# Large SBUF buffers laid out ahead of the small ones, so that TensorE's operands start at multiples of 512 bytes

## The chip, the cores and the metric

One NeuronCore of a Trainium2 chip runs one program. The metric is device time in microseconds (us). Before the change the median of three runs is 1743.22 us, with 1742.43 and 1743.45 us at the ends. The profiled execution took 1742.54 us, of which 1740.5 us lie between its first and its last instruction (its span).

## The reference

Chunked attention feeds a dense two-layer network, which feeds a mixture of eight experts:

```python
# q, k, v: 8 batches, 8 heads, 576 rows of 64; attention inside chunks of 64 rows
scores = scale * q_c @ k_c.T ; scores -= max
attn = exp(scores) / (sum + 1e-9)
x = (attn @ v_c) -> 4608 tokens x 512
h = x @ w_in ; x = (h - tanh(h)) @ w_out          # 512 -> 2048 -> 512
noisy = x @ w_gate + log1p(exp(x @ w_noise)) * noise
top 2 of 8 experts for each token, softmax over the two
out += weight * (relu(x[mask] @ w1[e]) @ w2[e])   # 512 -> 1024 -> 512, for each expert
```

All of it is float32. The kernel reaches float32 accuracy with three matmuls where one would do: each operand is split into a high part, rounded to the format `fp32r`, and a low part that holds the rest, and high x high, high x low and low x high are summed in PSUM.

## The kernel before

**Tiling.** A token tile is 128 tokens, and 36 tiles make 11 groups of the first network: 4, 3, 4, 3, 4, 3 tiles, and then five groups of 3. For each group the kernel runs 16 steps, one for each 128 hidden units. A step is a first layer (`products1`, line 331: 12 matmuls, each of 512 or 384 columns, as many as the group has tokens) and a second layer (`products2`, line 439: 3 matmuls for each token tile, each of 512 columns). The experts follow with the same two lines: 8 experts, each with three groups of 512, 384 and at most 352 tokens (in another order for odd and even experts), 8 steps for a group. Where an expert got so few tokens that its last tile is empty, the group of 352 runs as 256.

**Software pipeline.** `advance` issues the first layer of a step, and then the second layer of the step before it. Thus matmuls of line 331 and of line 439 alternate in blocks. Between blocks there are slots, filled by an explicit table, in which the attention of later tiles, the gating and the preparation of weights are issued. In the part of the experts TensorE runs the two lines alone.

**The four operands.** A matmul has a stationary operand (`lhsT`, loaded by an LDWEIGHTS instruction) and a moving operand (`rhs`, streamed):

```python
nc.tensor.matmul(s.hp[:, :n], lhsT=w[:, a, d, :], rhs=s.xt[:, b, d, :n], ...)            # line 331
nc.tensor.matmul(s.grp["acc"][j][:m], lhsT=s.gt[:, a, j * 128:j * 128 + m],
                 rhs=s.B[s.f][:, b, :], ...)                                               # line 439
```

In the first layer the stationary operand is a weight tile `wa` (128 columns of 4 bytes, thus 512 bytes in a partition), the moving one is the transposed input `xt`. In the second layer the stationary one is the activation `gt`, the moving one is the weight tile `wb`. `xt` is two buffers: groups with an even number use `xt0` (512 columns to a part), odd ones `xt1` (384 columns). `gt` is two buffers in rotation. The last group's eight steps are different: their activations are kept, under the name `gl`, in buffers of the tag `wa`, and their second layer runs at the very end, tile by tile (`by_tiles`), first the tile of 96 tokens and then the two of 128.

**Where a tile lies.** A pool gives its buffers their addresses in the order in which their tags are first asked for. In the pool `sp` the sixteen `wa`, the sixteen `wb` and three working buffers come first. What follows is asked for as the program comes to it, and small tiles (`mx`, 2 x 32 bytes, and `sm`, 2 x 32 bytes) are asked for between large ones. Addresses are bytes within a partition.

Of the kernel before, what the change touches and what calls it, by code (L numbers as in the profile page):

```python
# [10 lines left out]
F32R = mybir.dt.float32r  # L11
# [19 lines left out]
def moe_chain_kernel(ctx: ExitStack, tc: tile.TileContext, q, k, v, w_in, w_out, wgn, noise,  # L31
# [15 lines left out]
    sp = ctx.enter_context(tc.tile_pool(name="sp", bufs=1))  # L47
# [46 lines left out]
    def blk(name, tag, bufs, dt=F32):  # L94
        return sp.tile([128, 512], dt, name=name, tag=tag, bufs=bufs)
# [7 lines left out]
    def spare(tag, f):  # L103
        return raws[tag][f].bitcast(F32)
# [13 lines left out]
    def load_v(i):  # L118
        V[i] = spare("wb", NF1 - 2)[:, i % 2] if 2 <= i < GS[0] else blk("v", "v", 2)
        nc.sync.dma_start(V[i], v[i])  # L120

    PS, MX, PT, PX, LO = {}, {}, {}, {}, {}

# [70 lines left out]
    def p_mm(i):  # L194
        PX[i] = place_of(i, 0)
        products(PX[i], V.pop(i), PT.pop(i))
        if GS[0] <= i + 2 < NT:
            load_v(i + 2)
# [40 lines left out]
    def u_p_chunk(i, c):  # L239
        if c == 0:  # L240
            PX[i] = one_bank()
        products(PX[i], V[i], PT[i], (c,))
        g, j = place[i]
        if i == G0[g] and c == 0:
            XT[g] = new_xt(g, 128 * GS[g])
        s0 = j * 128 + 64 * c
        hi, lo = [XT[g][:, b, :, s0:s0 + 64] for b in range(2)]
        nc.scalar.copy(hi, PX[i][:, c])
        nc.vector.tensor_tensor(lo, PX[i][:, c], hi.bitcast(F32), op=ALU.subtract)
        if c == 1:  # L250
            for d in (V, PT, PX):
                d.pop(i)
            load_v(i + 2)
# [570 lines left out]
    for i in range(GS[0]):  # L824
        load_q(i)
        load_k(i)
        if i == 1:
            load_v(0)
# [249 lines left out]
    for g in range(NG):  # L1078
        h0 = H1 * g
        at(h0, load_nz, g)  # L1080
        if g > 0:
            n = GS[g - 1]
# [177 lines left out]
```

## Time and profile before

| | |
|---|---|
| median of three runs | 1743.22 us |
| profiled execution | 1742.54 us |
| its span | 1740.5 us |
| TensorE busy with matmuls | 1728.3 us (99%) |
| TensorE loading weights | 1485.9 us (85%) |
| VectorE, ScalarE, GpSimd busy | 790.6, 547.5, 491.7 us |
| DMA | 184.68 MB, mean 106 GB/s |

How to read it: matmuls are pipelined, so the duration of one (some 395 ns for 512 columns) overlaps the next ones, and a busy TensorE says nothing of its rate. The rate is read from the timeline, which merges instructions of one kind that follow each other: the start of a block, taken from the start of the next block, over the number of matmuls in it is the time from one matmul to the next, called the pitch here.

### The profile page before, as it was taken

What the parts mean: (1) busy time and instruction counts of PE and PEld (TensorE: products, weight loads), DVE (VectorE), ACT (ScalarE), POOL (GpSimd) and SP (SyncE); (2) the same over time, 40 slices, a digit from 0 to 9 for tenths busy, and PEclk for the clock granted to TensorE, in tenths of its full rate; (3) what the DMA queues carried; (4) which work ended last, traced back from release to release, by engine and by line L of the source; (5) the groups of instructions that cost most, each with busy time, mean ns of one, the idle gap of its engine ahead of it and who ended that gap; (6) DMA issues with size and microseconds to landing.
All of it is one profiled execution on the core that took longest, in us unless ns stands there. A gap on an engine that the chain in (4) does not pass through costs nothing.

```text
span 1740.5 us, 28351 instructions
## 1 busy us (share of the span) xinstructions
PE 1728.3 (99%) x10776; PEld 1485.9 (85%) x10777; DVE 790.6 (45%) x2070; ACT 547.5 (31%) x1108; POOL 491.7 (28%) x752
## 2 busy tenths in 40 slices
PE   8999999999999999999999999999999999999998
PEld 6788888888888888888898888988898888988887
DVE  8866443644454544544465333434333333343321
ACT  5643322332232333323342323323223222232211
POOL 4640403040304213031253523222232222232112
PEclk9999999999999999999999999999999999999999
DMA  8546525571323222121354543543354353443312
GB/s 315 182 128 161 163 63 155 126 206 43 107 79 113 82 79 101 55 95 38 112 175 120 130 108 79 106 106 68 87 103 104 73 96 85 93 111 71 65 25 37
DMA packets 197830, 184.68 MB, mean 106 GB/s; under 512 B 80176, under 2 KB 139568, under 8 KB 197680
## 3 DMA queue, kind: packets, MB, share of 16 engines
q1 hardware_dynamic: 178064, 142.73, 27.5%
q0 software_dynamic: 19328, 39.41, 11.8%
q8 instruction: 96, 1.57, 0.4%
q14 instruction: 54, 0.44, 0.1%
q10 hardware_dynamic: 288, 0.52, 0.1%
HBM read 118.76 MB, written 63.84 MB: 105 GB/s over the span
## 4 chain that ended last, share of the span: by engine, by line
PE 97%; DVE 1%; ACT 0%; POOL 0%; issue 0%; POOLq 0%; ACTq 0%; DVEq 0%
PE hp L331 47%; PE acc L439 46%; PE pair L136 2%; PE pt L190 1%; PE one L136 0%; PE pair L538 0%; PE acc L519 0%; PE hp L820 0%; DVE sm L172 0%; DVE e L156 0%; PE pair L519 0%; POOL out_dram L794 0%; DVE mx L149 0%; DVE g L370 0%; ACT xt L206 0%
## 5 line engine op out<-in xcount | busy, mean ns | idle before, releaser
L331 PE MATMUL hp<-xt,wa 128*128 128x384 f32 (+3 forms) x4416 | 879.3, 348 | 0.9 <-ACT xt L206 0.9
L439 PE MATMUL acc<-wb,gt 128*128 128x512 f32 x3432 | 859.0, 395 | 0.0
L331 PEld LDWEIGHTS hp<-xt,wa 128*128 128x128 f32 x4416 | 765.2, 188 | 82.9 <-issue 2.6
L439 PEld LDWEIGHTS acc<-wb,gt 128*128 128x128 f32 x3432 | 636.3, 188 | 131.0
L378 DVE SCALAR_TENSOR_TENSOR gt<-hp,gt 128x384 fp32r<-128x384 f32 (+2 forms) x184 | 109.2, 593 | 437.3 <-ACT gt L375 437.3
L375 ACT ACTIVATE gt<-hp 128x384 fp32r<-128x384 f32 (+2 forms) x184 | 95.6, 520 | 445.9 <-PE hp L331 426.0
L370 DVE TENSOR_TENSOR g<-hp,g 128x384 f32<-128x384 f32 (+1 forms) x176 | 104.1, 592 | 249.9 <-ACT g L367 249.3
L367 ACT ACTIVATE g<-hp 128x384 f32<-128x384 f32 (+1 forms) x176 | 91.4, 519 | 335.5 <-PE hp L331 330.8
L316 POOL TENSOR_TENSOR wb<-st,wb 128x512 fp32r<-128x512 f32 x64 | 92.9, 1451 | 321.5 <-ACT wb L314 321.5
L373 DVE TENSOR_TENSOR gt<-g,gt 128x384 fp32r<-128x384 f32 (+1 forms) x160 | 94.1, 588 | 96.0 <-ACT gt L371 95.5
L371 ACT CAST gt<-g 128x384 fp32r<-128x384 f32 (+1 forms) x176 | 95.4, 542 | 130.3 <-DVE g L370 116.2
L794 POOL DMA_INDIRECT out_dram<-o,lsa x73 | 119.3, 1634 | 53.4 <-DVE o L791 31.3
L396 POOL COPY spacer<-mark 1x1 f32<-1x1 f32 x182 | 47.2, 260 | 304.3 <-DVE mark L391 237.8
L613 POOL TENSOR_SCALAR r<-d 128x3 f32<-128x3 f32 (+1 forms) x11 | 3.3, 297 | 425.5 <-ACT d L604 425.4
L664 POOL DMA_INDIRECT xs<-yr,row x72 | 71.2, 988 | 32.0 <-issue 25.1
L269 DVE TENSOR_TENSOR xt<-xg,xt 128x512 fp32r<-128x512 f32 x80 | 54.3, 679 | 54.7 <-ACT xt L268 54.7
L268 ACT CAST xt<-xg 128x512 fp32r<-128x512 f32 x80 | 48.8, 610 | 91.6 <-DVE xg L491 90.1
L664 POOL DMA_INDIRECT lst<-pay,row x72 | 70.2, 975 | 16.1 <-issue 14.0
L491 DVE STREAM_TRANSPOSE xg<-xg 128x512 f32<-128x512 f32 x80 | 56.3, 704 | 0.0
L316 DVE TENSOR_TENSOR wa<-st,wa 128x512 fp32r<-128x512 f32 x64 | 44.1, 688 | 5.5 <-ACT wa L314 5.4
L314 ACT CAST wa<-st 128x512 fp32r<-128x512 f32 x64 | 39.3, 613 | 4.6 <-DMA st<-in_w_dram 4.6
L314 ACT CAST wb<-st 128x512 fp32r<-128x512 f32 x64 | 39.7, 620 | 0.4 <-DMA st<-in_w_dram 0.4
(197 smaller groups left out, 896.3 us busy)
## 6 DMA issues: line engine op xcount, KB each, us to landing
st<-in_w_dram SPq DMA_DIRECT2D x128, 256.0 KB, 2.9
xg<-xs SPq DMA_DIRECT2D x320, 64.0 KB, 2.4
out_dram<-zero SPq DMA_DIRECT2D x40, 256.0 KB, 4.5
x2d<-y SPq DMA_DIRECT2D x36, 256.0 KB, 2.3
z<-x2d SPq DMA_DIRECT2D x144, 64.0 KB, 2.1
yr<-x2d SPq DMA_DIRECT2D x36, 256.0 KB, 4.5
q<-in_q_dram SPq DMA_DIRECT2D x34, 256.0 KB, 4.1
v<-in_v_dram SPq DMA_DIRECT2D x34, 256.0 KB, 3.6
```

The source lines that it names most:

```text
L314: nc.scalar.copy(w[:, 0, :], x)
L316: eng.tensor_tensor(w[:, 1, :], x, w[:, 0, :].bitcast(F32), op=ALU.subtract)
L331: nc.tensor.matmul(s.hp[:, :n], lhsT=w[:, a, d, :], rhs=s.xt[:, b, d, :n], start=(i == 0), stop=(i == 11))
L367: nc.scalar.activation(g, hp[:, :n], AF.Tanh)
L370: nc.vector.tensor_tensor(g, hp[:, :n], g, op=ALU.subtract)
L371: nc.scalar.copy(hi, g)
L373: eng.tensor_tensor(lo, g, hi.bitcast(F32), op=ALU.subtract)
L375: nc.scalar.activation(hi, hp[:, :n], AF.Relu)
L378: nc.vector.scalar_tensor_tensor(lo, hp[:, :n], 0.0, hi.bitcast(F32), op0=ALU.max, op1=ALU.subtract)
L439: nc.tensor.matmul(s.grp["acc"][j][:m], lhsT=s.gt[:, a, j * 128:j * 128 + m], rhs=s.B[s.f][:, b, :], start=(s.f == 0 and i == 0), stop=(s. ...
L664: s = nc.gpsimd.indirect_dma_start(out=to, out_offset=bass.IndirectOffsetOnAxis(ap=at, axis=0), in_=src, in_offset=None)
L794: a = nc.gpsimd.indirect_dma_start(out=out, out_offset=bass.IndirectOffsetOnAxis(ap=en[:m, 0:1], axis=0), in_=o[:m], in_offset=None, compu ...
```

## The change

Five requests for tiles are put ahead of the small ones. The tiles that they return are not used: the requests only fix where the tags lie.

```diff
@@ -118,6 +118,12 @@
     def load_v(i):
         V[i] = spare("wb", NF1 - 2)[:, i % 2] if 2 <= i < GS[0] else blk("v", "v", 2)
         nc.sync.dma_start(V[i], v[i])
+
+    for n, m in ((0, 512), (1, 384)):
+        sp.tile([128, 2, 4, m], F32R, name=f"xt{n}", bufs=1)
+    sp.tile([128, 2, 512], F32R, name="gt", bufs=2)
+    blk("e", "e", 2)
+    blk("y", "y", 4)
 
     PS, MX, PT, PX, LO = {}, {}, {}, {}, {}
```

The built program holds the same instructions on each engine, in the same order, with the same waits and the same shapes. Every buffer keeps its users; what differs is the address of these (the small ones, of 4 to 128 bytes, move behind them):

| buffer | bytes | address before | mod 512 | address after | mod 512 |
|---|---|---|---|---|---|
| `wa` x16, `wb` x16, `xg`/`ks`/`pts` | 4096 each | 19456 to 158720 | 0 | the same | 0 |
| `xt0` | 16384 | 187520 | 128 | 162816 | 0 |
| `xt1` | 12288 | 212480 | 0 | 179200 | 0 |
| `gt` x2 | 4096 each | 203904, 208000 | 128 | 191488, 195584 | 0 |
| `e` x2 | 2048 each | 175168, 177216 | 64 | 199680, 201728 | 0 |
| `y` x4 (also `z`, `x`, `o`, `yr`, `x2t`) | 2048 each | 179328 to 185472 | 128 | 203776 to 209920 | 0 |
| `g`, `q` x2, `v` x2, `x2t` | 2048 each | 162816 to 173056 | 0 | 211968 to 222208 | 0 |

## Rows read from the trace of the kernel before

**Rows 1.** The page, part 1: busy us (share of the span) and instructions.

```profile
PE 1728.3 (99%) x10776; PEld 1485.9 (85%) x10777; DVE 790.6 (45%) x2070; ACT 547.5 (31%) x1108; POOL 491.7 (28%) x752
```

**Rows 2.** The page, part 4: the chain that ended last, by engine.

```profile
PE 97%; DVE 1%; ACT 0%; POOL 0%; issue 0%; POOLq 0%; ACTq 0%; DVEq 0%
```

**Rows 3.** TensorE's waits: who waited for whom, us in total, times, longest.

```profile
PE hp L820 <- DVE warm L814: 1.3, 1, 1.3
...
PE pair L136 <- DMA wa<-in_k_dram: 0.4, 1, 0.4
```

**Rows 4.** Groups of TensorE's matmuls by shape: count | busy us, mean ns.

```profile
L439 PE MATMUL acc<-wb,gt 128*128 128x512 f32 x3408 | 855.8, 395 | 0.0
...
L331 PE MATMUL hp<-xt,wa 128*128 128x352 f32 x192 | 32.3, 322 | 0.0
...
L439 PE MATMUL acc<-wb,gl 128*128 128x512 f32 x48 | 11.0, 389 | 0.0
```

**Rows 5.** TensorE's timeline, experts' groups of 384 and 512: start us, us, what.

```profile
1317.31 2.27 PE L331 MATMUL hp<-xt,wa 128*128 128x384 f32 x12
1319.42 2.25 PE L439 MATMUL acc<-wb,gt 128*128 128x512 f32 x9
1321.51 2.27 PE L331 MATMUL hp<-xt,wa 128*128 128x384 f32 x12
...
1352.98 2.96 PE L331 MATMUL hp<-xt,wa 128*128 128x512 f32 x12
1355.78 2.96 PE L439 MATMUL acc<-wb,gt 128*128 128x512 f32 x12
1358.57 2.96 PE L331 MATMUL hp<-xt,wa 128*128 128x512 f32 x12
```

**Rows 6.** TensorE's timeline at the end (the second from 1722.5 us on).

```profile
1716.72 16.57 PE L439 MATMUL acc<-wb,gl 128*96 128x512 f32 x72
...
1722.25 11.04 PE L439 MATMUL acc<-wb,gl 128*128 128x512 f32 x48
```

**Rows 7.** TensorE's timeline from 1318.7 us: the last six of that block.

```profile
1318.38 1.20 PE L331 MATMUL hp<-xt,wa 128*128 128x384 f32 x6
```

**Rows 8.** TensorE's timeline, first network, a block of 384 that reads xt0.

```profile
757.58 2.27 PE L331 MATMUL hp<-xt,wa 128*128 128x384 f32 x12
759.69 2.26 PE L439 MATMUL acc<-wb,gt 128*128 128x512 f32 x9
```

**Rows 9.** TensorE's timeline: where experts 2 and 4 begin.

```profile
1107.85 2.27 PE L331 MATMUL hp<-xt,wa 128*128 128x384 f32 x12
...
1309.62 2.27 PE L331 MATMUL hp<-xt,wa 128*128 128x384 f32 x12
```

**Rows 10.** Stretches: length, PE, PEld, DVE, ACT, POOL busy (instructions), PEclk, DMA.

```profile
1107.85:1309.62 201.77, 201.77 (x1010) 173.91 (x1009) 72.67 (x164) 59.43 (x116) 56.88 (x56) 1.00 0.43 94
50.00:100.00 50.00, 50.00 (x321) 39.04 (x320) 41.93 (x79) 30.58 (x58) 31.88 (x26) 1.00 0.53 189
```

**Rows 11.** Timeline in the first group: TensorE, and GpSimd's weight preparation.

```profile
65.25 3.05 PE L439 MATMUL acc<-wb,gt 128*128 128x512 f32 x12
68.13 2.95 PE L331 MATMUL hp<-xt,wa 128*128 128x512 f32 x12
...
63.66 1.29 POOL L316 TENSOR_TENSOR wa<-x,wa 128x512 fp32r<-128x512 f32 x1 [0.32 <-ACT wa L314]
66.85 1.30 POOL L373 TENSOR_TENSOR gt<-g,gt 128x512 fp32r<-128x512 f32 x1 [1.90 <-ACT gt L371]
```

**Rows 12.** TensorE's timeline, blocks of 352: xt1, and then xt0.

```profile
1386.54 2.10 PE L331 MATMUL hp<-xt,wa 128*128 128x352 f32 x12
1388.48 2.96 PE L439 MATMUL acc<-wb,gt 128*128 128x512 f32 x12
...
1703.42 13.46 PE L331 MATMUL hp<-xt,wa 128*128 128x352 f32 x84
```

## The prediction

> **What bounds the kernel now.** The page's busy shares come first: matmuls keep TensorE busy for 1728.3 us, 99% of the span, and no other engine passes 45% [rows 1]. The chain that ended last says the same from the other side: 97% of it is TensorE [rows 2]. Then TensorE's waits: the longest is 1.3 us, for the very first operand, and the only one on a transfer is 0.4 us [rows 3]. So the kernel ends when TensorE has pushed its matmuls through, and the one thing worth asking is the pitch, the time from one matmul to the next. The clock was granted in full, the 2.4 GHz level, in the stretches that I use [rows 10], so a matmul of n columns streams for n / 2.4 ns: 213.3 ns for 512, 160.0 ns for 384.
>
> The pitch is read from block starts. In the experts' groups of 512 a first-layer block of 12 and a second-layer block of 12 take 1358.57 - 1352.98 = 5.59 us: 232.9 ns a matmul, 19.6 ns over the streaming time. In a group of 384 the 12 of the first layer take 1319.42 - 1317.31 = 2.11 us (175.8 ns, 15.8 over) and the 9 of the second layer 2.09 us (232.2 ns, 18.9 over) [rows 5]. These excesses are not waits; they are there in every block.
>
> Two places show another pitch. At the very end the last 48 matmuls take 11.04 us from the first start to the last end; less the 0.389 us of the last one [rows 4] that is 10.65 us for 47 pitches: 226.6 ns, 13.3 over [rows 6]. These are the same second-layer matmuls with the same `wb`, but the stationary operand is `gl`, which lies at a multiple of 512 bytes, while `gt` lies 128 bytes past one. And in the group of 384 that reads `xt1` (`xt1` and `wa` both at multiples of 512) the first six of a block take 1318.38 - 1317.31 = 1.07 us, 178.3 ns each, but the last six 1.04 us, 173.3 ns each, again 13.3 over [rows 5, 7]; the first six follow second-layer matmuls that loaded a `gt` out of place. A block that reads `xt0` (128 past) stays at 2.11 us for 12 [rows 8]. My reading: with both operands at multiples of 512 the excess settles at 13.3 ns; with one 128 bytes off it wanders around 16 to 20 ns.
>
> **The change part by part.** No instruction, wait or queue place is added or moved; only addresses differ. Three kinds of edits follow.
>
> *gt, xt0 and xt1.* Every first-layer and second-layer matmul then has both operands at multiples of 512. The term is (pitch now - settled pitch) x count, with 226.6 ns for 512 columns, 173.3 for 384, and by the same 13.3 over streaming 160.0 for 352 and 120.0 for 256. Before the change no row shows 512 columns in the first layer with `xt` in place, so there the 226.6 of the end is carried over. Its bounds: at most the 6.3 ns down to 226.6 plus another 2 ns, since one block (352 columns on `xt0`) runs as low as 11.6 over; at the other end 3.4 ns worse (the slower case below).
>
> - Experts. From the start of expert 2 to that of expert 4 lie 201.77 us [rows 9], in which TensorE runs lines 331 and 439 alone: 192 first-layer matmuls each of 512, 384 and 256 columns and 432 of the second layer, 1008 in all (1010 with the two cut by the edges) [rows 10]. Settled they take 624 x 226.6 + 192 x 173.3 + 192 x 120.0 = 141.4 + 33.3 + 23.0 = 197.7 us. That is 4.1 us less for two experts, 16.2 us for eight.
> - First network. A step of a group of four has 24 matmuls of 512: 24 x (232.9 - 226.6) = 0.151 us, and 3 x 16 = 48 steps give 7.3 us. A step of three has 4.20 us [rows 5] against 12 x 173.3 + 9 x 226.6 = 4.12 us: 0.081 us, and 8 x 16 = 128 steps give 10.4 us. Together 17.6 us. Here attention and gating put small matmuls between the blocks, and the block behind them carries a stumble of its own that stays: 12 second-layer matmuls take 68.13 - 65.25 = 2.88 us in the first group [rows 11], against 2.80 in the experts [rows 5]. The steps touched by this gain less, and I take four fifths: 14 us.
>
> *e, y and the buffers that share their tags.* VectorE, ScalarE, GpSimd and the DMA queues work on them. None of these is on the chain for 2% [rows 2], so a change of either sign in their durations is hidden behind matmuls: zero, up to 1 us either way for the transposes and attention products.
>
> *The small buffers, and `g`, `q`, `v`, `x2t`.* The latter were at multiples of 512 and stay so. Zero.
>
> **What could be late next.** A faster TensorE leaves the others less time. The tightest place is the first group, where VectorE is busy for 41.93 of 50 us [rows 10] decoding weights. There GpSimd has finished the weight tile of a later step at 64.95 us, and its first use is at 68.13 [rows 11]: 3.2 us of cover, while the whole group would gain 16 x 0.15 = 2.4 us. GpSimd also waits 1.90 us for the activation that TensorE feeds [rows 11], so it is itself paced by TensorE. I charge nothing; if the cover were used up, at most these 2.4 us would be lost.
>
> **The sum.** 16.2 + 14 = 30 us from the profiled execution's 1742.54 gives 1712.5 us; the median of the runs is 0.7 us higher. I forecast 1713 us.
>
> **The rivals.**
>
> *Half of it.* Lying in place may not be enough to settle. For it: the last group's 24 matmuls with a stationary operand of 96 columns take 1722.25 - 1716.72 = 5.53 us, 230.4 ns each, though both operands lie at multiples of 512 [rows 6]; and a block of 352 on `xt1`, in place, takes 1388.48 - 1386.54 = 1.94 us, 161.7 ns, 15.0 over [rows 12]. If blocks that follow small matmuls, 256 columns or 96-column tiles do not settle, some half of the gain is left: 1728 us. Against it: behind the 96-column tiles the 48 of 128 columns run at 226.6.
>
> *Nothing.* The 226.6 at the end could come from quiet: by then the other engines have almost no work in SBUF, and the address would not matter. Then the second layer keeps 232 and the time stays at 1743 us, within 1 or 2. Against it: the last six of the block in [rows 7] settle in the middle of the experts, with VectorE, ScalarE and GpSimd each busy for about 30% [rows 10], while the first layer on `xt0` with 512 columns never does.
> The Trainium skill, page "TensorE: Matmul & The Clock Gate", section "Step-by-step: what each phase is for", also speaks for nothing: the streamed operand and the weight load have a read port each, so loading the next weights takes no read bandwidth from the running matmul, and where the two operands lie relative to each other should be free. The same page, section "Wait — 56ns, not 53.3ns?", puts consecutive warm matmuls at the streaming time plus about 2.5 ns. The trace does not agree with that figure in any block: 13.3 ns at best, 19.6 in the groups of 512 [rows 5, 6]. By that rule the sum would be zero; by the rows it is 30 us.
>
> *Slower.* Operands that all start alike could meet in the same part of the memory on every pass. For it: 84 matmuls of 352 columns on `xt0`, out of place, take 1716.72 - 1703.42 = 13.30 us, 158.3 ns each [rows 6, 12], 3.4 ns less than the block on `xt1`, in place, at 161.7. If that is the rule and the other rows the exception, the 3408 second-layer matmuls [rows 4] and the 2304 of the first layer that read `xt0` (6 of 11 groups with 16 blocks of 12, 12 of 24 with 8) lose 3.4 ns each: 19.4 us, 1762 us. It decides if the step of 512 comes out above 5.59 us. Against it: the in-place block followed out-of-place `gt` loads, and the counts of 352 are small (192 [rows 4]).
>
> *The change does not do what it says.* The requests stand before the program's first small ones in that pool, and the addresses of the built program are those of the table; I give it no chance of its own.
>
> **How the numbers follow.** The forecast, a gain of 25 to 36 us (1707 to 1718), 0.62. Half of it, a gain of 8 to 25 us, 0.22. Nothing, 0.10. Slower, 0.06. A measurement of this kernel tells a change from none at about 0.2%, 3.5 us. Faster by more than that is the first two: 0.84; within it 0.10; slower 0.06. The range takes the forecast's own 1707 to 1718, a microsecond below it for excesses under 13.3 ns, and reaches up into the half case until no more than two tenths are left out: 1706 to 1733.
>
> **What would show it.** The experts' step of 512 takes 5.44 us instead of 5.59, the step of 384 4.12 instead of 4.20, and two experts 197.7 us instead of 201.8. First- and second-layer blocks of 12 with 512 columns both take 2.72 us. A block of 384 takes 2.08 us from its first matmul on. The blocks of 352 on `xt0` get slightly longer (160 ns a matmul, from 158.3). The last 48 matmuls do not change. The prediction fails if the second layer keeps 232 ns with `gt` in place (the end is special then), if only one of the two layers settles, or if TensorE shows waits on weights in the first 100 us.

## The result, and the profile after

The changed kernel takes 1726.05 us (median of five runs, 1725.13 to 1726.58) against 1743.22 us for the kernel before in the same comparison: a ratio of 0.9902, 95% interval 0.9891 to 0.9912. The profiled execution has a span of 1723.1 us, 17.4 us shorter than before. It is faster, by a little over half of what was forecast.

The page still describes the same kernel: the same number of instructions, and TensorE bound [rows 1, 2]. VectorE, ScalarE and GpSimd are busy for the same time within 1 us. Busy us (share) and instructions, then the chain that ended last:

```profile
PE 1710.9 (99%) x10776; PEld 1484.3 (86%) x10777; DVE 790.0 (46%) x2070; ACT 547.5 (32%) x1108; POOL 490.7 (28%) x752
...
PE 97%; DVE 1%; ACT 0%; POOL 0%; issue 0%; POOLq 0%; ACTq 0%; DVEq 0%
```

So the time went inside TensorE's own sequence, and the blocks tell where. By shape (count | busy us, mean ns), two groups of the kernel before beside [rows 4], and then the same three of the changed one:

```profile
L331 PE MATMUL hp<-xt,wa 128*128 128x384 f32 x2304 | 438.6, 338 | 0.0
L331 PE MATMUL hp<-xt,wa 128*128 128x512 f32 x1344 | 331.9, 395 | 0.9 <-ACT xt L206 0.9
...
L445 PE MATMUL acc<-wb,gt 128*128 128x512 f32 x3408 | 846.3, 393 | 0.0
L337 PE MATMUL hp<-xt,wa 128*128 128x384 f32 x2304 | 437.7, 338 | 0.0
L337 PE MATMUL hp<-xt,wa 128*128 128x512 f32 x1344 | 324.5, 390 | 0.9 <-ACT xt L212 0.9
```

The second layer is 9.5 us shorter, the first layer of 512 columns 7.4 and that of 384 columns 0.9. TensorE's timeline in the same experts as [rows 5] (start us, us, what; lines 337 and 445 are 331 and 439 of before):

```profile
1313.34 2.27 PE L337 MATMUL hp<-xt,wa 128*128 128x384 f32 x12
1315.44 2.24 PE L445 MATMUL acc<-wb,gt 128*128 128x512 f32 x9
1317.53 0.51 PE L337 MATMUL hp<-xt,wa 128*128 128x384 f32 x2
...
1340.29 2.88 PE L337 MATMUL hp<-xt,wa 128*128 128x512 f32 x12
1343.01 2.88 PE L445 MATMUL acc<-wb,gt 128*128 128x512 f32 x12
1345.72 0.39 PE L337 MATMUL hp<-xt,wa 128*128 128x512 f32 x1
```

In the group of 512 a step now takes 1345.72 - 1340.29 = 5.43 us, 226.3 ns a matmul; it was 5.59 [rows 5]. That is the settled step of 5.44 us within a hundredth. In the group of 384 a step takes 1317.53 - 1313.34 = 4.19 us, where 4.12 was forecast and 4.20 was there before. The second layer's 9 matmuls take 2.09 us, as before, although `gt` is in place now. The next block's last six and what follows, from a narrower window:

```profile
1318.59 1.20 PE L337 MATMUL hp<-xt,wa 128*128 128x384 f32 x6
1319.63 0.63 PE L445 MATMUL acc<-wb,gt 128*128 128x512 f32 x2
```

The first six take 1318.59 - 1317.53 = 1.06 us, 176.7 ns each, and the last six 1.04 us, 173.3 ns each: the picture of [rows 5, 7] with both operands of every matmul in place.

The sums agree. Where experts 2 and 4 begin, and where the first network begins and ends:

```profile
19.33 0.96 PE L337 MATMUL hp<-xt,wa 128*128 128x512 f32 x3 [0.91 <-ACT xt L212]
...
896.41 0.87 PE L337 MATMUL hp<-xt,wa 128*128 128x384 f32 x4
...
1098.19 1.05 PE L337 MATMUL hp<-xt,wa 128*128 128x384 f32 x5
...
1297.31 0.87 PE L337 MATMUL hp<-xt,wa 128*128 128x384 f32 x4
```

Two experts take 199.12 us instead of 201.77 [rows 9]: 2.65 less, where 4.06 was forecast. Of the first network the same two starts in the kernel before are these:

```profile
19.57 0.73 PE L331 MATMUL hp<-xt,wa 128*128 128x512 f32 x2 [0.91 <-ACT xt L206]
...
903.55 0.69 PE L331 MATMUL hp<-xt,wa 128*128 128x384 f32 x3
```

877.08 us instead of 883.98: 6.9 less, where 14 was forecast. Summed over both traces from block start to block start, the 112 steps of 512 columns gave 14.4 us (9.2 for the 64 in the experts, 5.2 for the 48 in the first network) and the 192 steps of 384 gave 2.9. The prediction had 10.4 + 64 x 0.081 = 15.6 us for these, before its discount; the 12.7 us that are missing here are as much as the whole gap between the gain forecast, 30, and the gain measured.

### The profile page after: what moved, and what is told of

Same layout as the page of the kernel before. It is cut to its first block, busy times and chain, and to the rows that moved or that the text cites. A ratio compares the mean times of both kernels' runs of the same rounds, so it can differ in the third digit from the quotient of the medians.

```text
span 1723.1 us, 28351 instructions
## 1 busy us (share of the span) xinstructions
PE 1710.9 (99%) x10776; PEld 1484.3 (86%) x10777; DVE 790.0 (46%) x2070; ACT 547.5 (32%) x1108; POOL 490.7 (28%) x752
## 3 DMA queue, kind: packets, MB, share of 16 engines
q8 instruction: 96, 1.57, 0.4%
## 4 chain that ended last, share of the span: by engine, by line
PE 97%; DVE 1%; ACT 0%; POOL 0%; issue 0%; POOLq 0%; ACTq 0%; DVEq 0%
PE hp L337 47%; PE acc L445 46%; PE pair L142 2%; PE pt L196 1%; PE one L142 0%; PE pair L544 0%; PE acc L525 0%; PE hp L826 0%; DVE sm L178 0%; DVE e L162 0%; PE pair L525 0%; POOL out_dram L800 0%; DVE mx L155 0%; DVE g L376 0%; ACT xt L212 0%
## 5 line engine op out<-in xcount | busy, mean ns | idle before, releaser
L337 PE MATMUL hp<-xt,wa 128*128 128x384 f32 (+3 forms) x4416 | 871.3, 346 | 0.9 <-ACT xt L212 0.9
L445 PE MATMUL acc<-wb,gt 128*128 128x512 f32 x3432 | 849.6, 393 | 0.0
L337 PEld LDWEIGHTS hp<-xt,wa 128*128 128x128 f32 x4416 | 764.9, 188 | 75.4 <-issue 2.6
L445 PEld LDWEIGHTS acc<-wb,gt 128*128 128x128 f32 x3432 | 635.2, 188 | 123.3 <-POOL wb L322 0.2
```

## The experiments

Times are set against the kernel before on the same chip in the same comparison; it took 1743.38 us beside e1 to e4, 1750.22 beside e5 to e7 and 1743.41 beside e8 and e9. The diffs show the main lines; `...` and comments stand for what is cut. In the rows the first layer is L337, L338, L342 or L343, the second L445, L446, L450 or L451, as lines above them were added.

### Which buffer: gt alone, xt0 alone

```diff
-    for n, m in ((0, 512), (1, 384)):                # after: xt0, xt1, gt, e, y
+    # e1: xt0, xt1, e, y, g, q, v, x2t, then mx and sm (128 bytes), then gt
+    # e2: xt1, gt, e, y, g, q, v, x2t, then mx and sm (128 bytes), then xt0
```

> As the changed kernel, but gt lies 128 bytes past a multiple of 512 again; xt0, xt1, e, y, g, q, v and x2t stay at multiples of 512. Theory A (a matmul settles at 13.3 ns over streaming only where both of its operands are in place, and each layer's own operands decide): the second layer goes back to 2.80 us for 12 matmuls and loses its 9.5 us, the first layer of 512 columns starts each block with some unsettled matmuls and loses a part of its 7.4 us: 1737 to 1741 us. Rival B (the two layers are independent: a block does not feel how the one before it lay): the first layer keeps 2.72 us for 12, only 9.5 us are lost: 1735.5 us. Rival C (it was xt alone): stays at 1726.

Measured: 1738.88 us, ratio 0.9974 (0.9964 to 0.9984). One step of 512 columns and the block behind it:

```profile
1349.84 2.92 PE L343 MATMUL hp<-xt,wa 128*128 128x512 f32 x12
1352.60 2.96 PE L451 MATMUL acc<-wb,gt 128*128 128x512 f32 x12
1355.39 2.92 PE L343 MATMUL hp<-xt,wa 128*128 128x512 f32 x12
```

The second layer is back at 2.79 us (2.80 before), and the first layer, whose own operands are in place, takes 2.76 instead of 2.72. Theory A holds, and its range too; rival B, for which layers do not feel each other, falls.

> As the changed kernel, but xt0 lies 128 bytes past a multiple of 512 again; gt, xt1 and the rest stay in place. Theory A: the first layer on xt0 loses its 7.4 us, and the second layer of the groups of 512, which starts each block behind it, loses a part of its gain: 1735 to 1741 us; blocks of 12 in these groups 2.80 us in the first layer and between 2.72 and 2.80 in the second. Rival B (layers independent): second-layer blocks keep 2.72 us, 1733.5 us. Rival C (it was gt alone): stays at 1726.

Measured: 1734.26 us, ratio 0.9947 (0.9930 to 0.9963).

```profile
1341.45 2.96 PE L343 MATMUL hp<-xt,wa 128*128 128x512 f32 x12
1344.24 2.90 PE L451 MATMUL acc<-wb,gt 128*128 128x512 f32 x12
1346.97 2.26 PE L343 MATMUL hp<-xt,wa 128*128 128x512 f32 x9
```

2.79 us for the first layer, 2.73 for the second. The time lies between A's range, which began at 1735, and B's 1733.5, so by time alone this does not decide: what the second layer takes over from the first is a hundredth of a microsecond a block here. Both buffers carry a part, and neither is enough.

### In place, or in place relative to each other

```diff
+    sp.tile([128, 32], F32, name="shift", bufs=1)
     raws = {tag: [sp.tile([128, 2, 512], U32, name=f"{tag}{f}", tag=tag, bufs=16)
```

> As the changed kernel, but a tile of 128 bytes stands ahead of all others in the pool, so wa, wb, xg, xt0, xt1, gt, e, y and the rest all lie 128 bytes past a multiple of 512. Theory D (what counts is where the two operands of a matmul lie relative to each other): no change against the changed kernel, 1726 us within 2, and 2.72 us for a block of 12 with 512 columns. Theory E (what counts is the multiple of 512 itself): back to the kernel before or worse, 1743 us and 2.80 us a block.

Measured: 1726.01 us, ratio 0.9901 (0.9884 to 0.9917).

```profile
1338.52 2.88 PE L446 MATMUL acc<-wb,gt 128*128 128x512 f32 x12
1341.24 2.88 PE L338 MATMUL hp<-xt,wa 128*128 128x512 f32 x12
1343.96 2.20 PE L446 MATMUL acc<-wb,gt 128*128 128x512 f32 x9
```

No large tile of the pool lies at a multiple of 512, and all is as in the changed kernel. What counts is the distance between a matmul's two operands. Theory E falls, and with it the multiple of 512 as a reason: it worked because both operands were then equally far from one.

### Which distances

```diff
+    # xt1, e, y, g, q, v, x2t as after; then a spacer; then gt and xt0
+    sp.tile([128, 4, 8], F32, name="nz", bufs=2)          # e5: 256 bytes
+    sp.tile([128, 2, 4, 1], F32, name="mx", bufs=2)       # e7: 64 bytes
```

> As the changed kernel, but xt0 and both gt lie 256 bytes past a multiple of 512; xt1 and the rest stay in place. Theory D2 (every offset between the two operands but 0 mod 512 unsettles): groups of 512 at about 2.80 us for 12 matmuls, time 1738 to 1746 us. Rival H (the pattern has a period of 256 bytes or less, and 128 was the bad offset): 2.72 us and 1726 us. An offset that settles lower than 13.3 ns is open too: some blocks of 352 columns with an offset of 128 stand at 11.6.

Measured: 1732.32 us in one run, 0.990 of the 1750.22 us of the kernel before beside it.

```profile
1347.30 2.88 PE L342 MATMUL hp<-xt,wa 128*128 128x512 f32 x12
1350.02 2.88 PE L450 MATMUL acc<-wb,gt 128*128 128x512 f32 x12
1352.74 0.61 PE L342 MATMUL hp<-xt,wa 128*128 128x512 f32 x2
```

Rival H holds: a distance of 256 bytes settles at 2.72 us like one of 0. (The absolute 1726 us was missed; the kernel before, too, took 7 us more in this comparison.)

> As the changed kernel, but xt0 and both gt lie 64 bytes past a multiple of 512; xt1 and the rest stay in place. Theory D2 (every offset but 0 mod 512 unsettles): about 2.80 us for 12 matmuls of 512 columns, 1738 to 1746 us. Rival J (a small offset disturbs less): between 2.72 and 2.80 us, 1728 to 1736 us.

Measured: 1747.77 us in one run, 0.9986 of the kernel before beside it.

```profile
1359.03 2.92 PE L342 MATMUL hp<-xt,wa 128*128 128x512 f32 x12
1361.79 2.96 PE L450 MATMUL acc<-wb,gt 128*128 128x512 f32 x12
1364.59 0.62 PE L342 MATMUL hp<-xt,wa 128*128 128x512 f32 x2
```

2.76 and 2.80 us: 64 bytes unsettle, in the second layer as much as 128 and in the first by half of it. The time in us was missed here too; by its ratio, 1741 us beside a kernel of 1743, it lies in D2's range and not in J's, though J's 2.72 to 2.80 us covers the first layer. For 512 columns no tried distance of `gt` and `xt0` runs below 2.72 us.

### What was left of the excess

```diff
+            c = 384 if s.kind == 2 and s.f and s.n in (384, 512) else 512
-            nc.tensor.matmul(s.grp["acc"][j][:m], lhsT=..., rhs=s.B[s.f][:, b, :], ...)
+            nc.tensor.matmul(s.grp["acc"][j][:m, :c], lhsT=..., rhs=s.B[s.f][:, b, :c], ...)
```

> As the changed kernel, but in the experts' groups of 512 and of 384 the second layer of steps 2 to 8 computes 384 of its 512 output columns (the last 128 columns keep the sum of the first step alone). So in the groups of 384 both layers stream 384 columns, and in the groups of 512 the first streams 512 and the second 384. Theory F (what is left of the excess comes from the change of column count between blocks): the groups of 384 settle, 12 first-layer matmuls 2.08 us and 9 second-layer ones 1.56, a step of 3.64 us; the groups of 512, settled at 2.72 us for 12 in the changed kernel, come unsettled: 2.75 us or more for the first layer, 2.11 or more for 12 of the second where 2.08 would be settled. Rival G (it belongs to 384 columns, to xt's spacing or to the first layer): the first layer of 384 stays at 2.10 to 2.11 us and the first layer of 512 at 2.72.

Measured (its 1671.44 us has less work in it and is not compared). A step of the group of 384, and then one of the group of 512:

```profile
1293.42 2.24 PE L337 MATMUL hp<-xt,wa 128*128 128x384 f32 x12
1295.50 1.72 PE L446 MATMUL acc<-wb,gt 128*128 128x384 f32 x9
1297.06 1.20 PE L337 MATMUL hp<-xt,wa 128*128 128x384 f32 x6
...
1319.00 2.92 PE L337 MATMUL hp<-xt,wa 128*128 128x512 f32 x12
1321.76 2.27 PE L446 MATMUL acc<-wb,gt 128*128 128x384 f32 x12
1323.86 1.31 PE L337 MATMUL hp<-xt,wa 128*128 128x512 f32 x5
```

With 384 columns in both layers the first takes 2.08 us and the second 1.56, a step of 3.64: settled as a whole block. With 512 and 384 columns in turn the group that was settled is not any more: 2.76 us instead of 2.72, and 2.10 instead of the settled 2.08 (theory F had said 2.11 or more). Theory F holds on both sides but for that hundredth, and rival G falls: with the operands in place, the excess that stays is started by the change of column count between blocks.

### e and y

```diff
-    blk("e", "e", 2)
-    blk("y", "y", 4)
```

> As the changed kernel without its last two lines, so that e and y lie 64 and 128 bytes past a multiple of 512 as in the kernel before, and xt0, xt1 and gt in place. Theory (e and y are zero): the same as the changed kernel, ratio 0.989 to 0.991 to the kernel before. Rival (they carry a part of the gain): ratio 0.993 or more.

Measured: 1725.99 us, ratio 0.9899 (0.9883 to 0.9916). The two lines carry nothing; `xt0` and `gt` carry the gain.

### A kernel with fewer changes of column count

```diff
-SIZES = None                                    # groups of 4, 3, 4, 3, 4, 3, then five of 3
+SIZES = [4] * 9
-    ... tag="bd", bufs=3                         # ks, pts, xg; fetched three ahead
+    ... tag="bd", bufs=2                         # two ahead
-        m = 512 if par % 2 == 0 else 384         # xt1
+        m = 512
-    for i, h in zip(range(GS[0], sum(GS[:2])), (2, 6, 10)):
+    for i, h in zip(range(GS[0], sum(GS[:2])), (2, 5, 8, 11)):
-        at(h + 7, u_t, i)
+        at(h + (6 if h < 8 else 9), u_t, i)
+                    if f == E:
+                        at(h0 + 2 * f, zero_rows, xs[SEAL - 128:SEAL, :])
```

> The changed kernel with the first network in nine groups of four tiles (144 steps of 512 columns in both layers) where it had three of four and eight of three (48 steps of 512 and 128 of 384). For the room xt1 is made 512 wide and the buffers for the experts' inputs go from three to two (fetched two ahead, not three); one more tile of scratch rows is cleared, and the attention of the second group's four tiles is put closer together in the first group's slots. Theory F (the change of column count between blocks costs what is left): 24 tiles leave 128 steps of 4.18 us for 96 steps of 5.44 us, 535.0 for 522.2: 12.8 us less, 1713 us within 4; first-layer and second-layer blocks of 12 in 2.72 us throughout the first network, no new wait of TensorE over 1 us. Rival I (the tighter schedule gives it back): TensorE waits for attention in the first 200 us or for the experts' inputs, 1720 us or more.

Measured: 1747.88 us, ratio 0.9979 (0.9969 to 0.9990). TensorE's largest wait (us in total, times, longest), then its timeline behind the first and behind the fifth of the seven, and the stretch of the first of these blocks as in [rows 10]:

```profile
PE pair L525 <- DVE e L162: 19.3, 7, 2.8
...
156.46 4.60 PE L337 MATMUL hp<-xt,wa 128*128 128x512 f32 x12
160.90 2.89 PE L445 MATMUL acc<-wb,gt 128*128 128x512 f32 x12
...
562.00 3.03 PE L337 MATMUL hp<-xt,wa 128*128 128x512 f32 x12
564.87 2.88 PE L445 MATMUL acc<-wb,gt 128*128 128x512 f32 x12
...
156.50:159.80 3.30, 3.30 (x12) 2.62 (x9) 0.00 (x0) 0.59 (x1) 0.00 (x0) 0.50 1.19 267
```

Rival I holds: in seven groups the gating's products ask for the PSUM pair in the slot in which VectorE still reads an attention tile's scores from it. With groups of three tiles they had a free bank of their own. And the waits cost more than their 19.3 us. Behind six of the seven, each a standstill of TensorE of 2.75 or 2.76 us, the granted clock is 0.50, the 1.2 GHz level; there the next block of 12 takes 160.90 - 156.46 = 4.44 us. Behind the fifth, where the clock stays at 1.00, it takes 2.87. Six times these 1.57 us would be 9.4 (an estimate from the one place); with the 19.3 that makes 28.7 of the 29.7 us between the spans of the two profiles, 1748.0 and 1718.3. The mend moves the gating one to two slots back:

```diff
-                hs = (9, 11, 12, 13, 15, 17, 21, 22, 22, 26)
+                hs = (11, 13, 14, 15, 15, 17, 21, 22, 22, 26)
-                hs = (9, 11, 12, 13, 17, 18, 19, 20, 20, 25)
+                hs = (11, 13, 14, 15, 17, 18, 19, 20, 20, 25)
```

> The nine groups of four again, with the gating products of line 525 and the three steps behind them one to two slots later (11 to 15 in place of 9 to 13), so that they do not ask for the PSUM pair in the slot in which an attention tile's scores are still being read from it. That wait was 19.3 us in seven pieces in the kernel with nine groups. Theory F: with the wait gone the 12.8 us of the groups of 384 appear: 0.982 to 0.986 of the kernel before, TensorE waiting less than 8 us in all. Rival I (the tighter schedule gives it back elsewhere): the wait comes back under another name, ratio 0.990 or more.

Measured: 1719.93 us, ratio 0.9865 (0.9849 to 0.9882), faster than both kernels; its interval and the changed kernel's do not touch. The wait is gone, and the granted clock is 0.999 again (0.993 in e6). TensorE's waits add up to 8.1 us, a tenth over the expected 8. One of them:

```profile
PE acc L445 <- DVE o L797: 1.0, 1, 1.0
```

The median stands just above the range that theory F gave. The timeline: two blocks with nothing between, a block behind attention products, and the starts of the first network, of expert 0 and of expert 1:

```profile
19.79 0.73 PE L337 MATMUL hp<-xt,wa 128*128 128x512 f32 x2 [0.91 <-ACT xt L212]
...
306.03 2.88 PE L337 MATMUL hp<-xt,wa 128*128 128x512 f32 x12
308.75 2.88 PE L445 MATMUL acc<-wb,gt 128*128 128x512 f32 x12
311.47 0.84 PE L337 MATMUL hp<-xt,wa 128*128 128x512 f32 x3
...
334.86 3.04 PE L337 MATMUL hp<-xt,wa 128*128 128x512 f32 x12
337.73 2.88 PE L445 MATMUL acc<-wb,gt 128*128 128x512 f32 x12
...
887.83 0.87 PE L337 MATMUL hp<-xt,wa 128*128 128x384 f32 x4
...
993.67 0.62 PE L337 MATMUL hp<-xt,wa 128*128 128x512 f32 x2
```

Blocks of 2.72 us, as forecast. But the block behind attention products takes 2.87. Small matmuls are a change of column count too, but they also differ in shape and operands (64 x 64), so which of these makes the 0.15 us was not told apart. The first network takes 868.0 us, 9.0 less than in the changed kernel, of the 12.8 forecast. Not all of these are a matter of changes: its 96 steps have 384 first-layer matmuls fewer than the 128 that they replace, and at 13.3 ns over streaming each that is 5.1 us (an estimate from the settled pitch). And the first expert takes 105.84 us, where the changed kernel has 102.21 (its second expert begins at 998.62):

```profile
998.62 0.62 PE L337 MATMUL hp<-xt,wa 128*128 128x512 f32 x2
```

Those 3.6 us are given back while the last group, of four tiles now, is gated and dispatched. TensorE waits three times in this stretch, 1.9 us in all: 0.9 for gating and dispatch, and 1.0 for an output of the experts (`o`, above); in the changed kernel it does not wait there. Another 0.6 us is a border effect: the last step's second layer falls behind the border, and it has 12 matmuls now and not 9. No wait of TensorE is for an input tile, but VectorE waits 2.6 us for one here; whether the two input buffers have a part in the 1.0 us was not told apart.

## Why the prediction was right and wrong

- *What bounds it, and where the time would come from*: right. TensorE bound both kernels, and the gain lies in its pitch. That `gt` and `xt0` out of place cost it is shown by putting each back (e1, e2).
- *The 512-column steps*: right. 5.44 us forecast, 5.43 measured; the carry-over of 226.6 ns from the last blocks to a first layer that no row showed in place was good. What was not right is the condition, "both operands at multiples of 512": e3 has the same pitch with none there. The rival "nothing" falls: the settled pitch runs in the middle of the experts, beside the other engines' work, and 5.59 against 5.43 us with the same instructions is an effect of addresses alone. The trace does not agree with what the prediction drew from the Trainium skill, page "TensorE: Matmul & The Clock Gate", section "Step-by-step: what each phase is for", where the streamed operand and the weight load have a read port each: that their relative place should be free.
- *The 384-column steps*: here the prediction failed. The step was "the first six follow second-layer matmuls that loaded a `gt` out of place": I took an unsettled start for the mark of `gt`'s address, and so priced the steps of three tiles at 4.12 us. They take 4.19. The unsettled start comes from the change between 384 and 512 columns (e4), and the second layer of these groups, with its 9 matmuls, gains a hundredth of a microsecond from `gt` in place. Of the terms, the experts' steps of 512 gave 9.2 us of 9.7 and the first network's 5.2 of 7.3, somewhat less than the four fifths allowed for; the steps of 384 gave 2.9 of 15.6, and the experts' third groups nothing measurable of 1.3. The rows held a hint: a first-layer block of 384 takes 2.11 us on `xt1`, in place, and 2.11 on `xt0`, out of place [rows 5, 8].
- *The rival "half of it"*: this is what came out, in its time, 1728 us, and in its band, a gain of 8 to 25 us, which had 0.22. It had the right kind of cause, blocks in place that do not settle, but named the wrong blocks: 352 columns, 256 columns, 96-column tiles and small matmuls. Alternating 384 and 512 was the large case, with 192 steps, and the rows of before could not tell it from the address of `gt`, since in that kernel each such change came with a `gt` out of place. That 1726.05 us lies in the stated range, 1706 to 1733, is no merit of the sum, whose own 1707 to 1718 was missed: the range had been drawn into this rival's band.
- *"Slower"*: the row it rested on was real but small. The last group's 84 matmuls of 352 columns, in place now, take 13.53 us instead of 13.30 [rows 6, 12]. So 13.3 ns over streaming, which the prediction calls the best of any block, is not: out of place these had 11.6.

```profile
1685.76 13.69 PE L337 MATMUL hp<-xt,wa 128*128 128x352 f32 x84
1699.29 16.59 PE L445 MATMUL acc<-wb,gl 128*96 128x512 f32 x72
```

- *e, y and the rest at zero*: right (e8). No new wait appeared in the first 100 us either; TensorE's longest there is still 1.3 us.

## What to carry to other kernels

When a kernel is bound by a stream of float32 matmuls, read the pitch from block starts and compare it between blocks of the same shape: at the full granted clock, an excess over n / 2.4 ns that differs from block to block can be an effect of where the operands lie. Put a matmul's stationary and moving operand at a distance that is a multiple of 256 bytes (0 and 256 modulo 512 were tried here), then look whether neighbouring blocks have the same column count, and prefer tilings in which they do. And before pricing a difference, look for the second thing that is there with it: in the kernel before, every change between 384 and 512 columns came with a `gt` out of place. Last, a short standstill of TensorE can cost more than its length: look at the granted clock behind it (e6).

## What was not expected

- The distance between the two operands counts, not their alignment: all buffers moved by 128 bytes run like none (1726.01 us), and 256 bytes between the operands are as good as 0 (2.72 us a block), while 64 and 128 are not (2.79 to 2.80 in the second layer).
- A block passes its state on. A first layer in place behind a second layer out of place takes 2.76 instead of 2.72 us (e1), and a change of column count costs the steps of 384 0.07 us each even with all in place.
- What in the chip does this stays open. The rows show a settled pitch of 13.3 ns over streaming for 384 and 512 columns, and that a block of 384 behind one of 512 needs several matmuls to reach it (176.7 ns each for the first six, 173.3 for the last); no run here shows the part that makes them wait. Weight loads run beside matmuls (TensorE is busy 99% of the span with these and 86% with loads), so the distance that counts may be that to the operand of the matmul before; inside a block both have the same value, and no run tells them apart.
